# Group normalisation over 128 images: scaling shares put back on VectorE, and one load split over unequal DMA engines

## The chip, the core and the metric

The kernel runs on one core of one Trainium2 chip. The metric is the device time of one execution in microseconds (us). The core has TensorE (PE), VectorE (DVE), ScalarE (ACT), GpSimd (POOL) and SyncE (SP), and 16 DMA engines that move data between the device memory and the on-chip memory. In the profile a line number such as L368 is a line of the kernel.

## The reference

`x` has the shape (128, 1024, 32, 16) in bf16: 134 MB in, and as much out. Each image's 1024 channels form 32 groups of 32 channels. Each group of an image is normalised by its own mean and variance, and each channel is then scaled and shifted:

```
xr = x.reshape(B, G, C // G, H, W)                   # B=128, G=32
mu = xr.mean(axis=(2, 3, 4), keepdims=True)
var = ((xr - mu) ** 2).mean(axis=(2, 3, 4), keepdims=True)
xn = ((xr - mu) / sqrt(var + 1e-5)).reshape(B, C, H, W)
return xn * g[None, :, None, None] + b[None, :, None, None]
```

## The kernel before

The work is cut into 32 tiles (`NT`). A tile is four images: its 128 partitions are 4 images x 32 groups, and a partition holds one whole group, 32 channels of 512 values, which is a row of 16,384 bf16 values or 32 KB. A tile is thus 4 MB, loaded whole, changed in place and stored whole. Six buffers (`XBUFS`) rotate in `xpool`.

Loads and stores are all issued by SyncE. `L(i)` loads tile i. Six tiles are loaded up front; after that tile i+5 (`AHEAD`) is loaded after the store of tile i. Since its buffer is that of tile i-1, SyncE waits, before it issues the load, for the store of tile i-1 to have landed, and everything after it in SyncE's order waits too. The first and the last tile are loaded in four column quarters; the last two tiles are stored in quarters.

Order on every engine is fixed by `chain`, which ties each instruction to the one before it under the same key ("sp", "act", "dve", "pool", "pe"). The program writes that order out: for each tile i come `Q(i)`, `M(i+1)`, `R0(i+1)`, `V(i)`, `A(i)`.

- `M` sums the row on TensorE: 32 matmuls with an identity matrix (`eye`) add up the 32 blocks of 512 columns in PSUM (`pa`). Only the first and last tile (`shifted`) use two sums, `pa` of 8 matmuls and `pb` of 24.
- `R0` reduces that sum on VectorE to the negative mean (`negmean`, L189). For the two shifted tiles it is a quarter's estimate `q`, and `R1` adds the rest and forms a correction (`off`, `seed`) on GpSimd.
- `Q` squares the row on ScalarE with a running sum, in two halves of 8192 values whose unused outputs are FP8 (`ja`, L244). Between the halves stands `finish(i-1)`: ScalarE scales the last two channels of the tile before (`LAST_SHARE`, L363), the tile is stored and the next load issued. GpSimd then forms part of the variance (`v0`, L273).
- `V` takes the root on ScalarE and the reciprocal on VectorE (`rstd`, L312), and GpSimd forms the 32 factors and offsets of the channels (`scl` L337, `shift` L343, `bia` L353).
- `A` scales and shifts the channels in place (L368): channels 0 to 21 on VectorE, and 22 to 29 on GpSimd (`POOL_SHARE` = 8). The tile before the last is scaled wholly on VectorE, the last one on VectorE and ScalarE.

Of the kernel before, what the change touches and what calls it, by code (L numbers as in the profile page):

```python
# [8 lines left out]
ACT = mybir.ActivationFunctionType  # L9
# [3 lines left out]
FP8 = mybir.dt.float8e5  # L13
# [11 lines left out]
LAST_SHARE = 2  # L25
POOL_SHARE = 8
# [3 lines left out]
def kernel(  # L30
# [62 lines left out]

    def L(i):
        xt = xpool.tile([P, F], BF16, name="xt")
        parts = NQ if i == 0 or i >= NT - 1 else 1
        w = F // parts
        for c in range(parts):
            chain(
                "sp",  # L100
                nc.sync.dma_start(  # L101
                    out=xt[:, c * w : (c + 1) * w], in_=x_v[i][:, c * w : (c + 1) * w]
                ),
            )
        state[i] = {"xt": xt}

    for i in range(min(UPFRONT, NT)):
        L(i)

# [48 lines left out]
    def shifted(i):  # L158
        return i == 0 or i == NT - 1

    def matmuls(st, name, lo, hi):
        ps = pspool.tile([P, MMN], F32, name=name)
        for k in range(lo, hi):
            chain(
                "pe",
                nc.tensor.matmul(  # L166
                    out=ps[:],
                    lhsT=eye[:],
                    rhs=st["xt"][:, k * MMN : (k + 1) * MMN],
                    start=(k == lo),  # L170
                    stop=(k == hi - 1),
                ),
            )
        st[name] = ps

    def M(i):
        st = state[i]
        if shifted(i):
            matmuls(st, "pa", 0, MQ)
            matmuls(st, "pb", MQ, NMM)  # L180
        else:
            matmuls(st, "pa", 0, NMM)
# [18 lines left out]
    def R0(i):  # L201
        st = state[i]
        if shifted(i):
            st["q"] = sum_of(st["pa"], None, "q")
        else:
            st["negmean"] = sum_of(st["pa"], None, "negmean")

    def R1(i):
        st = state[i]
        if not shifted(i):  # L210
            return
# [3 lines left out]
            "pool",  # L215
            nc.gpsimd.tensor_scalar(  # L216
# [10 lines left out]
            "pool",  # L227
            nc.gpsimd.tensor_scalar(
                out=seed[:],
                in0=off[:],  # L230
                scalar1=-1.0,
                scalar2=off[:],
# [6 lines left out]
    def squares(st, w, k, bias, scale, sq):  # L239

        ja = jpool.tile([P, F // 2], FP8, name="ja")
        chain(
            "act",
            nc.scalar.activation(  # L244
                out=ja[:, 0:w],
                in_=st["xt"][:, k * w : (k + 1) * w],
                func=ACT.Square,
                bias=bias,
                scale=scale,
                accum_out=sq,  # L250
                saturate=False,
            ),
        )

    def Q(i):

        st = state[i]
        if shifted(i):
            sq = spool.tile([P, NQ], F32, name="sq")
            for k in range(NQ):  # L260
                squares(st, QF, k, st["q"][:], 1.0 / NQ, sq[:, k : k + 1])
                if k == 0:
                    finish(i - 1)
            st["sq"] = sq
            return
        s0 = spool.tile([P, 1], F32, name="s0")
        s1 = spool.tile([P, 1], F32, name="s1")
        squares(st, F // 2, 0, st["negmean"][:], 1.0, s0[:])
        v0 = spool.tile([P, 1], F32, name="v0")
        finish(i - 1)  # L270
        chain(
            "pool",
            nc.gpsimd.tensor_scalar(  # L273
                out=v0[:],
                in0=s0[:],
                scalar1=inv_n,
                scalar2=EPS,
                op0=ALU.mult,
                op1=ALU.add,
            ),  # L280
        )
        squares(st, F // 2, 1, st["negmean"][:], 1.0, s1[:])
        st["v0"], st["s1"] = v0, s1

    def V(i):
        st = state[i]
        if shifted(i):
            var = spool.tile([P, 1], F32, name="var")
            jv = spool.tile([P, NQ], F32, name="jv")
            chain(  # L290
                "dve",
                nc.vector.tensor_scalar(  # L292
                    out=jv[:],
                    in0=st["sq"][:],
                    scalar1=inv_n,
                    scalar2=st["seed"][:],
                    op0=ALU.mult,
                    op1=ALU.add,
                    accum_out=var[:],
                ),  # L300
            )
            last_sum, scale, bias = var, float(NQ * NQ), eps_t
        else:
            last_sum, scale, bias = st["s1"], inv_n, st["v0"]
        rstd = spool.tile([P, 1], F32, name="rstd")
        chain(
            "act",
            nc.scalar.activation(  # L308
                out=rstd[:], in_=last_sum[:], func=ACT.Sqrt, bias=bias[:], scale=scale
            ),  # L310
        )
        chain("dve", nc.vector.reciprocal(out=rstd[:], in_=rstd[:]))  # L312
        scl = spool.tile([P, KC], F32, name="scl")
        bia = spool.tile([P, KC], F32, name="bia")
        if i == NT - 1:
            chain(
                "dve",
                nc.vector.tensor_scalar(
                    out=scl[:], in0=gam, scalar1=rstd[:], scalar2=None, op0=ALU.mult
                ),  # L320
            )
            chain(
                "dve",
                nc.vector.scalar_tensor_tensor(  # L324
                    out=bia[:],
                    in0=scl[:],
                    scalar=st["negmean"][:],
                    in1=bet,
                    op0=ALU.mult,
                    op1=ALU.add,  # L330
                ),
            )
        else:
            shift = spool.tile([P, KC], F32, name="shift")
            chain(
                "pool",
                nc.gpsimd.tensor_scalar(  # L337
                    out=scl[:], in0=gam, scalar1=rstd[:], scalar2=None, op0=ALU.mult
                ),
            )  # L340
            chain(
                "pool",
                nc.gpsimd.tensor_scalar(  # L343
                    out=shift[:],
                    in0=scl[:],
                    scalar1=st["negmean"][:],
                    scalar2=None,
                    op0=ALU.mult,
                ),
            )  # L350
            chain(
                "pool",
                nc.gpsimd.tensor_tensor(out=bia[:], in0=shift[:], in1=bet, op=ALU.add),  # L353
            )
        st["scl"], st["bia"] = scl, bia

    def scale_on(key, i, k):
        st = state[i]
        span = st["xt"][:, k * HW : (k + 1) * HW]
        scl = st["scl"][:, k : k + 1]  # L360
        bia = st["bia"][:, k : k + 1]
        if key == "act":
            inst = nc.scalar.activation(  # L363
                out=span, in_=span, func=ACT.Identity, bias=bia, scale=scl
            )
        else:
            eng = nc.vector if key == "dve" else nc.gpsimd
            inst = eng.tensor_scalar(  # L368
                out=span,
                in0=span,  # L370
                scalar1=scl,
                scalar2=bia,
                op0=ALU.mult,
                op1=ALU.add,
            )
        chain(key, inst)
# [9 lines left out]

    def in_parts(i):
        return i >= NT - STORE_IN_PARTS

    def A(i):  # L390

        if not in_parts(i):
            for n in range(POOL_SHARE):
                scale_on("pool", i, KC - LAST_SHARE - POOL_SHARE + n)
            for k in range(KC - LAST_SHARE - POOL_SHARE):
                scale_on("dve", i, k)
            if i + 1 < NT:
                R1(i + 1)
            return
        for c in range(NQ):  # L400
            for k in range(c * KQ, (c + 1) * KQ):
                on_act = i == NT - 1 and k >= (c + 1) * KQ - ACT_SHARE
                scale_on("act" if on_act else "dve", i, k)
            S(i, c, c + 1)
            if c == NQ // 2 - 1 and i + 1 < NT:
                R1(i + 1)

    def finish(i):
        if i < 0 or in_parts(i):
            return  # L410
        for k in range(KC - LAST_SHARE, KC):
            scale_on("act", i, k)
        S(i, 0, NQ)
        state.pop(i)
        j = i + AHEAD
        if UPFRONT <= j < NT:
            L(j)
# [5 lines left out]
    for i in range(NT):  # L423
# [5 lines left out]
        A(i)  # L429
# [30 lines left out]
```

## Time and profile before

| What | Value |
|---|---|
| Time, median of 3 runs | 635.33 us (635.27 to 635.8) |
| The profiled execution's own time | 635.33 us |
| Its span, first to last instruction | 633.4 us |
| Bytes over the span | 268.69 MB at 424 GB/s |
| Busy: ScalarE | 518.1 us (82%) |
| Busy: VectorE | 368.9 us (58%) |
| Busy: TensorE | 289.4 us (46%) |
| Busy: GpSimd | 228.4 us (36%) |
| A load of 4 MB, issue to landing (median) | 29.2 us |
| A store of 4 MB, issue to landing (median) | 38.3 us |

Busy time is an average over the run: an engine may be the limit in one stretch and idle in the next. The queues of the DMA engines are listed by number in the page: q1 is SyncE's, q10 is the one that carried the two small loads of `g` and `b`, and q8 and q14 carry the engines' own instructions. Every row of a tile is one DMA packet. A transfer has landed when each of the DMA engines that worked on it has reported its share done.

### The profile page before, as it was taken

To read this page: it belongs to the slowest core of one execution; us is meant where nothing else is said; L and a number is where in the kernel's file an instruction comes from. 1 tells how busy PE (TensorE), PEld (TensorE's weight loads), DVE (VectorE), ACT (ScalarE), POOL (GpSimd) and SP (SyncE) were. 2 spreads that over 40 slices of the span, in tenths; PEclk is the share of its full clock that TensorE was granted. 3 is DMA by queue.
4 is the path that set the end of the run, shared out by engine and by line. 5 is a ranking of instruction groups with operands and counts; after the bars stand their busy time and mean duration, and the time that the engine had idled before them with its cause. 6 is when DMAs were issued, how large, how long until landed. Compare 5 with 4: busy or idle time off the path is not lost.

```text
span 633.4 us, 3906 instructions
## 1 busy us (share of the span) xinstructions
PE 289.4 (46%) x1025; PEld 113.3 (18%) x1025; DVE 368.9 (58%) x825; ACT 518.1 (82%) x238; POOL 228.4 (36%) x373
## 2 busy tenths in 40 slices
PE   5577604663345633456423655235553355547000
PEld 2223201221112211122101222012221122212000
DVE  0077777767744577545675455754557645567760
ACT  4599999999977798777987788977879778797960
POOL 0044444444442244422444333443324433244100
PEclk9789758766787667876668776687866678668655
DMA  9999999999999999999999999999999999999995
GB/s 367 433 431 419 430 431 430 430 433 430 430 434 433 435 431 429 431 430 428 431 435 426 433 439 439 431 426 433 430 435 430 430 435 430 433 423 439 431 418 228
DMA packets 11062, 268.69 MB, mean 424 GB/s; under 512 B 1312, under 2 KB 1312, under 8 KB 1312
## 3 DMA queue, kind: packets, MB, share of 16 engines
q1 hardware_dynamic: 10944, 268.44, 98.8%
q8 instruction: 8, 0.13, 0.1%
q14 instruction: 14, 0.11, 0.0%
q10 hardware_dynamic: 96, 0.00, 0.0%
HBM read 134.22 MB, written 134.22 MB: 424 GB/s over the span
## 4 chain that ended last, share of the span: by engine, by line
DMA 71%; ACT 10%; PE 9%; DVE 3%; issue 3%; POOL 1%; SPq 0%; DVEq 0%; ACTq 0%; POOLq 0%
DMA out_dram<-xt 41%; DMA xt<-in_x_dram 30%; PE pa L166 9%; ACT ja L244 9%; DVE xt L368 3%; ACT xt L363 1%; SPq L101 0%; POOL scl L337 0%; PE pb L166 0%; POOL shift L343 0%; ACT rstd L308 0%; DVE jd L189 0%; DVE rstd L312 0%; POOL bia L353 0%; DVE jv L292 0%
## 5 line engine op out<-in xcount | busy, mean ns | idle before, releaser
L244 ACT ACTIVATE ja<-xt,negmean 128x8192 fp8e5<-128x8192 bf16 x60 | 426.7, 7112 | 74.7 <-DVE jd L189 74.7
L166 PE MATMUL pa<-xt,eye 128*128 128x512 bf16 x976 | 278.6, 456 | 294.6 <-DMA xt<-in_x_dram 294.6
L368 DVE TENSOR_SCALAR xt<-xt,scl,bia 128x512 bf16<-128x512 bf16 x716 | 341.3, 552 | 39.8 <-POOL bia L353 39.8
L166 PEld LDWEIGHTS <-eye 128*128 128x128 bf16 x1024 | 113.2, 113 | 470.8 <-DMA xt<-in_x_dram 295.9
L368 POOL TENSOR_SCALAR xt<-xt,scl,bia 128x512 bf16<-128x512 bf16 x240 | 190.5, 805 | 3.3
L337 POOL TENSOR_SCALAR scl<-gb,rstd 128x32 f32<-128x32 f32 x31 | 11.1, 358 | 337.0 <-DVE rstd L312 337.0
L189 DVE TENSOR_SCALAR_CACHE_REDUCE jd<-pa 128x512 bf16<-128x512 f32 x32 | 22.0, 688 | 172.3 <-PE pa L166 172.3
L363 ACT ACTIVATE xt<-xt,bia,scl 128x512 bf16<-128x512 bf16 x68 | 50.8, 798 | 0.8 <-DVE bia L324 0.8
L244 ACT ACTIVATE ja<-xt,q 128x4096 fp8e5<-128x4096 bf16 x8 | 29.7, 3708 | 7.0 <-DVE jd L189 6.8
L312 DVE RECIPROCAL rstd<-rstd 128x1 f32<-128x1 f32 x32 | 5.1, 160 | 24.6 <-ACT rstd L308 24.6
L343 POOL TENSOR_SCALAR shift<-scl,negmean 128x32 f32<-128x32 f32 x31 | 11.1, 358 | 3.1
L166 PE MATMUL pb<-xt,eye 128*128 128x512 bf16 x48 | 11.0, 379 | 1.0 <-DMA xt<-in_x_dram 1.0
L244 ACT ACTIVATION_READ_ACCUMULATOR ja<-xt,negmean 128x1 f32 x60 | 11.2, 186 | 0.0
L308 ACT ACTIVATE rstd<-s,v 128x1 f32<-128x1 f32 x30 | 8.8, 295 | 2.8
L353 POOL TENSOR_TENSOR bia<-shift,gb 128x32 f32<-128x32 f32 x31 | 7.8, 251 | 2.6
L216 POOL TENSOR_SCALAR off<-negmean,q 128x1 f32<-128x1 f32 x2 | 0.9, 430 | 20.6 <-DVE jd L189 20.6
L308 ACT ACTIVATE rstd<-var,eps_t 128x1 f32<-128x1 f32 x2 | 0.6, 294 | 7.5 <-DVE jv L292 7.5
L273 POOL TENSOR_SCALAR v<-s 128x1 f32<-128x1 f32 x30 | 5.7, 191 | 2.5
L156 DVE COPY gb<-gb_p 128x64 f32<-128x64 f32 x1 | 0.2, 225 | 5.3 <-PE gb_p L148 5.3
L116 ACT ACT_TABLE_LOAD x1 | 1.3, 1283 | 1.7 <-PEq L444 1.7
L189 DVE DVE_READ_ACCUMULATOR jd<-pa 128x1 f32 x32 | 2.6, 81 | 0.0
L292 DVE TENSOR_SCALAR_CACHE_REDUCE jv<-sq,seed 128x4 f32<-128x4 f32 x2 | 0.4, 216 | 2.9 <-ACT ja L244 2.9
(18 smaller groups left out, 6.1 us busy)
## 6 DMA issues: line engine op xcount, KB each, us to landing
xt<-in_x_dram SPq DMA_DIRECT2D x30, 4096.0 KB, 29.2
out_dram<-xt SPq DMA_DIRECT2D x30, 4096.0 KB, 38.3
xt<-in_x_dram SPq DMA_DIRECT2D x8, 1024.0 KB, 16.4
out_dram<-xt SPq DMA_DIRECT2D x8, 1024.0 KB, 18.8
gb_b<-in_g_dram ACTq DMA_DIRECT2D x1, 2.0 KB, 3.4
gb_b<-in_b_dram ACTq DMA_DIRECT2D x1, 2.0 KB, 5.4
```

Source lines behind the costliest of these rows:

```text
L116: chain("act", nc.scalar.activation(out=warm[:], in_=eps_t[:], func=ACT.Sqrt))
L166: nc.tensor.matmul(out=ps[:], lhsT=eye[:], rhs=st["xt"][:, k * MMN : (k + 1) * MMN], start=(k == lo), stop=(k == hi - 1),),
L189: nc.vector.tensor_scalar(out=jd[:], in0=ps[:], scalar1=-inv_n, scalar2=seed, op0=ALU.mult, op1=ALU.add, accum_out=total[:],),
L244: nc.scalar.activation(out=ja[:, 0:w], in_=st["xt"][:, k * w : (k + 1) * w], func=ACT.Square, bias=bias, scale=scale, accum_out=sq, satura ...
L273: nc.gpsimd.tensor_scalar(out=v0[:], in0=s0[:], scalar1=inv_n, scalar2=EPS, op0=ALU.mult, op1=ALU.add,),
L308: nc.scalar.activation(out=rstd[:], in_=last_sum[:], func=ACT.Sqrt, bias=bias[:], scale=scale),
L312: chain("dve", nc.vector.reciprocal(out=rstd[:], in_=rstd[:]))
L337: nc.gpsimd.tensor_scalar(out=scl[:], in0=gam, scalar1=rstd[:], scalar2=None, op0=ALU.mult),
L343: nc.gpsimd.tensor_scalar(out=shift[:], in0=scl[:], scalar1=st["negmean"][:], scalar2=None, op0=ALU.mult,),
L353: nc.gpsimd.tensor_tensor(out=bia[:], in0=shift[:], in1=bet, op=ALU.add),
L363: inst = nc.scalar.activation(out=span, in_=span, func=ACT.Identity, bias=bia, scale=scl)
L368: inst = eng.tensor_scalar(out=span, in0=span, scalar1=scl, scalar2=bia, op0=ALU.mult, op1=ALU.add,)
```

## The change

The scaling, the small arithmetic and the squares change place, and the load of one tile is issued differently.

- `A` scales all 32 channels of a tile on VectorE (in the last tile ScalarE keeps two of every eight). `POOL_SHARE`, `LAST_SHARE` and `finish` are gone, so the store and the next load are issued after `A(i)`.
- `V` and `R1` do their small arithmetic on VectorE: `scl`, `bia`, `off`, `seed`.
- Every tile is summed and squared the way the first and the last were: `pa` of 8 matmuls gives `q`, ScalarE squares four quarters of 4096 values around `q` with bf16 outputs, and `R1(i+1)`, which needs `pb`, stands in the middle of `A(i)`.
- The load of tile 16 is issued in four parts: rows 0 to 59 by GpSimd, and rows 60 to 123, 124 to 126 and 127 by SyncE. In the change's own words the 60 rows go over 15 DMA engines, sparing engine 3, and the others over 16, 3 and 1 engines.
- `turn(n)` is a small GpSimd load of n x 4 pieces of 4 bytes from `g`, whose data nothing uses. `turn(4)` is issued after the loads up front, `turn(13)` after the split load.

```diff
-FP8 = mybir.dt.float8e5
-LAST_SHARE = 2
-POOL_SHARE = 8
+SPLIT_TILE = 16
+WIDE = 60
+SPARED = 3
...
+    def turn(n):
+        t = consts.tile([n, 4, 4], BF16, name=f"turn{n}")
+        chain("pool", nc.gpsimd.dma_start(
+                out=t[:, :, 0:2],
+                in_=g[0 : n * 8].rearrange("(p a c) -> p a c", a=4, c=2)))
...
     def L(i):
         xt = xpool.tile([P, F], BF16, name="xt")
+        if i == SPLIT_TILE:
+            chain("pool", nc.gpsimd.dma_start(
+                    out=xt[0:WIDE, :], in_=x_v[i][0:WIDE, :], max_dma_last_dim=2 * F))
+            for lo, hi in ((WIDE, P - 4), (P - 4, P - 1), (P - 1, P)):
+                chain("sp", nc.sync.dma_start(out=xt[lo:hi, :], in_=x_v[i][lo:hi, :]))
+            turn(16 - SPARED)
+            state[i] = {"xt": xt}
+            return
...
     for i in range(min(UPFRONT, NT)):
         L(i)
+
+    turn(SPARED + 1)
...
     def M(i):
         st = state[i]
-        if shifted(i):
-            matmuls(st, "pa", 0, MQ)
-            matmuls(st, "pb", MQ, NMM)
-        else:
-            matmuls(st, "pa", 0, NMM)
+        for name, lo, hi in (("pa", 0, MQ), ("pb", MQ, NMM)):
...
     def Q(i):
+        sq = spool.tile([P, NQ], F32, name="sq")
+        for k in range(NQ):
+            ja = jpool.tile([P, QF], BF16, name="ja")
+            chain("act", nc.scalar.activation(out=ja[:],
+                    in_=st["xt"][:, k * QF : (k + 1) * QF], func=ACT.Square,
+                    bias=st["q"][:], scale=1.0 / NQ, accum_out=sq[:, k : k + 1]))
-        squares(st, F // 2, 0, st["negmean"][:], 1.0, s0[:])
-        finish(i - 1)
-        chain("pool", nc.gpsimd.tensor_scalar(out=v0[:], in0=s0[:], ...))
-        squares(st, F // 2, 1, st["negmean"][:], 1.0, s1[:])
...
     def V(i):
-        chain("pool", ...)      # scl, shift, bia
+        chain("dve", ...)       # scl, bia
...
+    def A(i, c):
+        for k in range(c * KQ, (c + 1) * KQ):
+            if i == NT - 1 and k >= (c + 1) * KQ - ACT_SHARE:
+                chain("act", nc.scalar.activation(...))
+            else:
+                chain("dve", nc.vector.tensor_scalar(...))
...
         V(i)
-        A(i)
+        in_parts = i >= NT - STORE_IN_PARTS
+        for c in range(NQ):
+            A(i, c)
+            if in_parts:
+                S(i, c, c + 1)
+            if c == NQ // 2 - 1 and i + 1 < NT:
+                R1(i + 1)
+        if not in_parts:
+            S(i, 0, NQ)
+        state.pop(i)
+        j = i + AHEAD
+        if UPFRONT <= j < NT:
+            L(j)
```

More of the change, by code (lines that the diff above doesn't have):

```diff
@@ L92 @@
     state = {}
+    def turn(n):
+        t = consts.tile([n, 4, 4], BF16, name=f"turn{n}")
+        chain(
+            "pool",
+            nc.gpsimd.dma_start(
+                out=t[:, :, 0:2],
+                in_=g[0 : n * 8].rearrange("(p a c) -> p a c", a=4, c=2),
+            ),
+        )
     def L(i):
         xt = xpool.tile([P, F], BF16, name="xt")
+        if i == SPLIT_TILE:
+            chain(
+                "pool",
+                nc.gpsimd.dma_start(
+                    out=xt[0:WIDE, :], in_=x_v[i][0:WIDE, :], max_dma_last_dim=2 * F
+                ),
+            )
+            for lo, hi in ((WIDE, P - 4), (P - 4, P - 1), (P - 1, P)):
+                chain(
+                    "sp", nc.sync.dma_start(out=xt[lo:hi, :], in_=x_v[i][lo:hi, :])
+                )
+            turn(16 - SPARED)
+            state[i] = {"xt": xt}
+            return
         parts = NQ if i == 0 or i >= NT - 1 else 1
@@ L156, in GB @@
         chain("dve", nc.vector.tensor_copy(out=gb[:], in_=gb_p[:]))
[L158 to L174, printed above, removed]
     def M(i):
         st = state[i]
-        if shifted(i):
-            matmuls(st, "pa", 0, MQ)
-            matmuls(st, "pb", MQ, NMM)
-        else:
-            matmuls(st, "pa", 0, NMM)
+        for name, lo, hi in (("pa", 0, MQ), ("pb", MQ, NMM)):
+            ps = pspool.tile([P, MMN], F32, name=name)
+            for k in range(lo, hi):
+                chain(
+                    "pe",
+                    nc.tensor.matmul(
+                        out=ps[:],
+                        lhsT=eye[:],
+                        rhs=st["xt"][:, k * MMN : (k + 1) * MMN],
+                        start=(k == lo),
+                        stop=(k == hi - 1),
+                    ),
+                )
+            st[name] = ps
     def sum_of(ps, seed, name):
@@ L201, in R0 @@
     def R0(i):
[L202 to L206, printed above, removed]
+        state[i]["q"] = sum_of(state[i]["pa"], None, "q")
     def R1(i):
         st = state[i]
-        if not shifted(i):
-            return
         st["negmean"] = sum_of(st["pb"], st["q"][:], "negmean")
@@ L214, in R1 @@
         chain(
-            "pool",
-            nc.gpsimd.tensor_scalar(
+            "dve",
+            nc.vector.tensor_scalar(
                 out=off[:],
@@ L226, in R1 @@
         chain(
-            "pool",
-            nc.gpsimd.tensor_scalar(
+            "dve",
+            nc.vector.scalar_tensor_tensor(
                 out=seed[:],
                 in0=off[:],
-                scalar1=-1.0,
-                scalar2=off[:],
+                scalar=-1.0,
+                in1=off[:],
                 op0=ALU.mult,
@@ L237, in R1 @@
         st["seed"] = seed
-    def squares(st, w, k, bias, scale, sq):
-        ja = jpool.tile([P, F // 2], FP8, name="ja")
-        chain(
[L243 to L251, printed above, removed]
-            ),
-        )
[L255 to L262, printed above, removed]
-                    finish(i - 1)
[L264 to L267, printed above, removed]
-        squares(st, F // 2, 0, st["negmean"][:], 1.0, s0[:])
[L269 to L281, printed above, removed]
-        squares(st, F // 2, 1, st["negmean"][:], 1.0, s1[:])
-        st["v0"], st["s1"] = v0, s1
@@ L285, in V, with Q @@
[L285 to L304, printed above, removed]
+    def Q(i):
+        st = state[i]
+        sq = spool.tile([P, NQ], F32, name="sq")
+        for k in range(NQ):
+            ja = jpool.tile([P, QF], BF16, name="ja")
+            chain(
+                "act",
+                nc.scalar.activation(
+                    out=ja[:],
+                    in_=st["xt"][:, k * QF : (k + 1) * QF],
+                    func=ACT.Square,
+                    bias=st["q"][:],
+                    scale=1.0 / NQ,
+                    accum_out=sq[:, k : k + 1],
+                ),
+            )
+        st["sq"] = sq
@@ L305, in V @@
+    def V(i):
+        st = state[i]
+        var = spool.tile([P, 1], F32, name="var")
+        jv = spool.tile([P, NQ], F32, name="jv")
+        chain(
+            "dve",
+            nc.vector.tensor_scalar(
+                out=jv[:],
+                in0=st["sq"][:],
+                scalar1=inv_n,
+                scalar2=st["seed"][:],
+                op0=ALU.mult,
+                op1=ALU.add,
+                accum_out=var[:],
+            ),
+        )
         rstd = spool.tile([P, 1], F32, name="rstd")
@@ L308, in V @@
             nc.scalar.activation(
-                out=rstd[:], in_=last_sum[:], func=ACT.Sqrt, bias=bias[:], scale=scale
+                out=rstd[:],
+                in_=var[:],
+                func=ACT.Sqrt,
+                bias=eps_t[:],
+                scale=float(NQ * NQ),
             ),
@@ L314, in V @@
         bia = spool.tile([P, KC], F32, name="bia")
[L315 to L372, printed above, removed]
+        chain(
+            "dve",
+            nc.vector.tensor_scalar(
+                out=scl[:], in0=gam, scalar1=rstd[:], scalar2=None, op0=ALU.mult
+            ),
+        )
@@ L373, in scale_on @@
+        chain(
+            "dve",
+            nc.vector.scalar_tensor_tensor(
+                out=bia[:],
+                in0=scl[:],
+                scalar=st["negmean"][:],
+                in1=bet,
                 op0=ALU.mult,
                 op1=ALU.add,
-            )
-        chain(key, inst)
+            ),
+        )
+        st["scl"], st["bia"] = scl, bia
+    def A(i, c):
+        st = state[i]
+        xt = st["xt"]
+        for k in range(c * KQ, (c + 1) * KQ):
+            span = xt[:, k * HW : (k + 1) * HW]
+            scl = st["scl"][:, k : k + 1]
+            bia = st["bia"][:, k : k + 1]
+            if i == NT - 1 and k >= (c + 1) * KQ - ACT_SHARE:
+                chain(
+                    "act",
+                    nc.scalar.activation(
+                        out=span, in_=span, func=ACT.Identity, bias=bia, scale=scl
+                    ),
+                )
+            else:
+                chain(
+                    "dve",
+                    nc.vector.tensor_scalar(
+                        out=span,
+                        in0=span,
+                        scalar1=scl,
+                        scalar2=bia,
+                        op0=ALU.mult,
+                        op1=ALU.add,
+                    ),
+                )
@@ L385, in S @@
         )
[L387 to L417, printed above, removed]
     M(0)
```

## The prediction

> **What bounds the kernel now.** I read the page's DMA parts first, then the chain of waits, SyncE's own waits, the tail of the run in stretches, and last the trace's completion records.
>
> ```profile
> span 633.4 us, 3906 instructions
> ...
> DMA  9999999999999999999999999999999999999995
> ...
> q1 hardware_dynamic: 10944, 268.44, 98.8%
> q8 instruction: 8, 0.13, 0.1%
> q14 instruction: 14, 0.11, 0.0%
> ```
>
> The DMA engines are full in 39 of 40 slices, and nearly all they carry is x in and out. No computing engine is as full (ACT 82%, DVE 58%). SyncE's own waits say the same: it waits for earlier stores to land and free a buffer, hardly for results.
>
> ```profile
> SPq L101 <- DMA out_dram<-xt: 451.3, 26, 19.5
> SPq L381 <- DVE xt L368: 125.7, 16, 36.8
> ```
>
> So time can only come from how many rows each DMA engine moves and what else it does. The last stretches (columns: length, five engines, clock, DMA share, GB/s) show how unevenly they finish:
>
> ```profile
> 620.00:622.00 2.00, 0.00 (x0) 0.00 (x0) 0.00 (x0) 0.00 (x0) 0.00 (x0) 0.50 1.01 426
> 622.00:624.00 2.00, 0.00 (x0) 0.00 (x0) 0.00 (x0) 0.00 (x0) 0.00 (x0) 0.50 0.96 406
> 624.00:626.00 2.00, 0.00 (x0) 0.00 (x0) 0.00 (x0) 0.00 (x0) 0.00 (x0) 0.50 0.62 262
> 626.00:628.00 2.00, 0.00 (x0) 0.00 (x0) 0.00 (x0) 0.00 (x0) 0.00 (x0) 0.50 0.26 111
> 628.00:630.00 2.00, 0.00 (x0) 0.00 (x0) 0.00 (x0) 0.00 (x0) 0.00 (x0) 0.50 0.13 53
> 630.00:632.00 2.00, 0.00 (x0) 0.00 (x0) 0.00 (x0) 0.00 (x0) 0.00 (x0) 0.50 0.06 25
> ```
>
> A share of 0.06 is one engine of 16: for the last 2 us a single engine works, at 25 GB/s. The trace also keeps, for each transfer, sixteen completion times, one per engine. For the transfers below, first completion (us) and how far behind it the six latest engines came:
>
> ```
>  22.27   0.38 0.39 0.40 0.42 0.43 0.59
>  71.45   0.41 0.42 0.44 0.50 2.03 2.70
> 216.73   1.55 1.60 2.64 3.58 4.16 4.34
> 313.55   2.51 2.56 3.41 4.45 5.08 5.95
> 400.71   2.74 3.36 3.97 4.37 5.01 6.90
> 623.75   2.34 3.28 3.39 4.41 5.04 6.27 8.65   (last transfer, seven latest)
> ```
>
> One engine loses 8.65 us on the fastest over the run, the next 6.27. It steps down where an 8 KB instruction packet lies. Packets of that size on q14 at 225.4, 313.5, 402.6, 499.1 and 593.2 us are each followed by a step of 0.78 to 0.97 us of the same last engine. They are about 90 us apart, 128 VectorE instructions; the other groups on q14 (three 160 to 180 us apart, three about 250 us) fit GpSimd and ScalarE. The packet takes 0.31 us, and the row after it is 0.38 to 0.66 us longer than the usual 1.213 us. From 4.34 behind at 217 us to 8.65 at the end, five packets: **0.86 us each**. The kernel ends when VectorE's instruction-fetching DMA engine ends.
>
> **Part by part.** *Scaling back on VectorE.* GpSimd's 240 scalings and 127 small operations, ScalarE's 60 scalings and both FP8 half-tile squares go; VectorE scales 32 channels a tile instead of 22 and does the small arithmetic.
>
> ```profile
> 575.27 10.77 DVE L368 TENSOR_SCALAR xt<-xt,scl,bia 128x512 bf16<-128x512 bf16 x22 [1.28 <-POOL bia L353]
> 575.34 6.35 POOL L368 TENSOR_SCALAR xt<-xt,scl,bia 128x512 bf16<-128x512 bf16 x8
> ...
> 591.54 5.25 DVE L368 TENSOR_SCALAR xt<-xt,scl,bia 128x512 bf16<-128x512 bf16 x16 [1.28 <-POOL bia L353]
> ```
>
> With GpSimd scaling beside it a VectorE scaling averages 0.49 us here (0.55 over the run); alone it takes 5.25/16 = 0.328. VectorE per tile: 32 x 0.328 = 10.5, two sums 0.69 + 0.74 with their read-outs 0.16, `jv` 0.30, `rstd` 0.16, `scl` 0.24, `bia` 0.25, `off` and `seed` at most the 0.43 and 0.29 that GpSimd took: 13.8 us. ScalarE: four squares of 3.71 + 0.19 and a root of 0.29: 15.9 us. A tile has two transfers of 9.71 us (first completions 22.27 and 31.98), 19.4 us. Both fit, so I cost the computing at nothing. Its cover is the DMA queue: the store issued at 280.41 had its last scaling at 272.7, 7.7 us of slack. The changed order needs only 8 of 32 matmuls (3.5 us instead of 9) before VectorE may go on, so stores become ready some 4 us earlier than now. If that cover were gone, every microsecond over 19.4 would count 31 times.
>
> *More VectorE instructions.* Section 1's 825 and 72 waits, branches and drains make 897 now; the built program has 1443. At one packet per 128, first at the 64th, that is 7 packets now and 11 after. Four more at 0.86: **+3.44 us** on the engine that is already last (bounds 4 x 0.78 = 3.1 and 4 x 0.97 = 3.9). GpSimd's packets vanish, but from engines that are not last: nothing for the end.
>
> [...]
>
> *The split load.* A row is 32 KB and costs its engine 9.71/8 = 1.214 us. A plain load gives each engine 8 rows. Now, by the change's words, 60 rows go as 4 rows on 15 engines, 64 as 4 on 16, and the last four as one each on three engines and one more on one. Engine 3 has 4 rows and saves 4 x 1.214 = **-4.86 us**; if the single row falls on one of the three, they have 10, 9 and 9, and pay 2.43, 1.21 and 1.21. Engine numbers are not in the trace; I take 3 to be the last engine, and the three to be none of the late ones, and weigh the contrary below.
>
> [...]
>
> *The second queue's own cost.* No data row goes from GpSimd now, so I bound it. Low: the 64-byte packets of `gb_b` on q10 between rows cost 0.01 us, and most 8 KB rows after them took 0.309, as elsewhere. High: each of the four rows lengthens the next one as an instruction packet does at its worst, 4 x 0.66 = 2.6 us on the fifteen engines. A gain is excluded: the bytes stay. I take 0.5, one lengthening, since the four follow one another. The next engine then stands at 6.27 + 0.5 = 6.8.
>
> *Waits and issues.* GpSimd's load waits for tile 10's store, as SyncE's did; only the small `turn(13)` queues behind it. Two more SyncE issues at about 0.35 us precede tile 12's store, which has the slack above. The first `turn` precedes `eye` on GpSimd and may hold up the first matmuls; tile 0's store, issued at 45.15 us, has loads ahead of it until 64 us.
>
> *Sum.* Last engine: 8.65 + 3.44 - 4.86 = 7.23 us behind, above 6.8, so it still ends last, 1.42 us sooner. Span 633.4 - 1.4 = 632.0; the profiled execution took 635.33, 1.93 more than its span, and equals the median of three: **633.9 us**.
>
> **Rivals.** *The second queue is dear.* If the fifteen pay 2.6, the second engine comes to 8.9 (+0.2); if the one at 6.27 is also loaded with 1.21 to 2.43 more, to 10.1 or 11.3: 635.6 to 638.0 us. For: the long rows after instruction packets. Against: q10's cheap packets.
>
> *The wrong engine is spared.* This ends slower. Then VectorE's fetches go unpaid: +3.44, 638.8 us (638.4 to 639.2). It decides if the engine without rows is any but the last one. For: no number in the trace ties it to 3. [...]
>
> *VectorE becomes the bound.* If scalings stayed at 0.552 us without GpSimd beside them, 32 of them and 3.3 us make 21 us a tile against 19.4: about 50 us more. The 0.328 rows speak against it.
>
> **Numbers.** Forecast 0.62, its own range 632.9 (the last engine is passed by the one at 6.27) to 635.4 (that engine is the one with two rows more, at 8.7); dear queue 0.18; wrong engine 0.17; VectorE 0.03. Low 632.9; high 638.8, since without half of the third case too much is left out. 0.2% is 1.27 us, about what can be told from no change. Of the forecast 0.38 lies below 634.06, 0.22 within and 0.02 above the bound; the dear queue gives 0.06 same and 0.12 slower; the others are slower.
>
> **What would show it.** Right: about fifteen q14 instruction packets; a GpSimd queue with 60 rows; VectorE scalings near 0.33 us; a last transfer whose engines spread over about 7.2 us, with the one-engine stretch shorter; tile 16's load short on one engine only. Wrong: the last engine steps down 11 times and never recovers (wrong engine); a common step of all but one engine near tile 16's load (dear queue); idle DMA slices mid-run (computing).

## The result, and the profile after

The changed kernel takes 646.3 us (median of 4 runs, 644.04 to 647.31) against 635.49 us for the kernel before on the same chip: 1.0165 times as long, 95% interval 1.0138 to 1.0192. The forecast was 633.9 us, with a range from 632.9 to 638.8. The profiled execution took 647.31 us with a span of 645.6 us, so the span grew by 12.2 us.

The page of the changed kernel, whose GB/s row has the moved bytes in 40 equal slices of 16.1 us:

```profile
span 645.6 us, 4013 instructions
...
GB/s 378 435 420 418 424 440 427 427 441 428 426 434 435 424 439 427 382 329 349 435 432 430 433 435 432 431 430 439 429 432 435 431 429 439 428 418 439 432 413 143
...
q1 hardware_dynamic: 10888, 266.47, 97.2%
q0 software_dynamic: 144, 1.97, 1.1%
q8 instruction: 8, 0.13, 0.1%
q14 instruction: 15, 0.12, 0.0%
```

Fifteen instruction packets on q14 and 1.97 MB (60 rows) on a new queue are as foreseen. Not foreseen are the slices 17 to 19, at 382, 329 and 349 GB/s where all others in the middle are near 431. Against 431 that is (49 + 102 + 82)/431 x 16.1 = 8.7 us of lost transfer. Tile 16's load is issued at 262 us, and the bytes fall from 268 us on. In stretches of 4 us (last two columns: DMA share, GB/s):

```profile
260.00:264.00 4.00, 0.95 (x5) 0.22 (x3) 3.93 (x14) 3.97 (x3) 1.17 (x2) 1.00 1.04 451
264.00:268.00 4.00, 0.00 (x0) 0.00 (x0) 4.00 (x14) 3.97 (x4) 0.00 (x0) 0.76 1.13 418
268.00:272.00 4.00, 0.00 (x0) 0.00 (x0) 1.21 (x4) 3.97 (x4) 0.00 (x0) 0.50 0.87 270
272.00:276.00 4.00, 0.00 (x0) 0.00 (x0) 0.00 (x0) 0.00 (x1) 0.00 (x0) 0.50 1.01 319
...
284.00:288.00 4.00, 4.00 (x14) 1.58 (x13) 1.89 (x9) 1.49 (x2) 0.00 (x0) 0.68 1.07 279
288.00:292.00 4.00, 3.31 (x16) 1.28 (x14) 4.00 (x14) 3.97 (x3) 0.00 (x0) 1.00 1.10 229
292.00:296.00 4.00, 0.00 (x0) 0.00 (x0) 3.93 (x14) 3.97 (x3) 0.00 (x0) 0.67 0.75 213
...
304.00:308.00 4.00, 4.00 (x20) 1.85 (x19) 3.53 (x14) 3.33 (x2) 0.00 (x0) 1.00 1.01 434
```

The DMA share stays near 1 (0.75 to 1.13 in these stretches) while the bytes fall to half: the engines are not short of work, each row takes longer. The packet records say the same. GpSimd's 60 rows, with rows of a store between them, took 1.9 us each in the median. Near 286 us, when they have all gone, most rows of SyncE's 64-row part take 2.48 to 2.50 us, and a few later ones up to 4.5, where a row elsewhere takes 1.213. Two dips of unlike make, one with GpSimd's queue and one without, are a first hint that the queue is not the cause.

At the end one engine works alone for longer than before, at 25 to 29 GB/s from 638 us on:

```profile
634.00:636.00 2.00, 0.00 (x0) 0.00 (x0) 0.00 (x0) 0.00 (x0) 0.00 (x0) 0.50 0.46 193
636.00:638.00 2.00, 0.00 (x0) 0.00 (x0) 0.00 (x0) 0.00 (x0) 0.00 (x0) 0.50 0.21 90
638.00:640.00 2.00, 0.00 (x0) 0.00 (x0) 0.00 (x0) 0.00 (x0) 0.00 (x0) 0.50 0.06 25
640.00:642.00 2.00, 0.00 (x0) 0.00 (x0) 0.00 (x0) 0.00 (x0) 0.00 (x0) 0.50 0.07 29
642.00:644.00 2.00, 0.00 (x0) 0.00 (x0) 0.00 (x0) 0.00 (x0) 0.00 (x0) 0.50 0.07 29
```

The sixteen completions of the last transfer now spread over 15.6 us instead of 8.65, and the last engine still steps back by about a microsecond after VectorE's instruction packets (from 5.24 to 6.24 us behind after the one at 242.1 us, from 16.30 to 17.26 after the one at 527.0).

### The profile page after: what moved, and what is told of

Same layout as the page of the kernel before. It is cut to its first block, busy times and chain, and to the rows that moved or that the text cites. A ratio compares the mean times of both kernels' runs of the same rounds, so it can differ in the third digit from the quotient of the medians.

```text
span 645.6 us, 4013 instructions
## 1 busy us (share of the span) xinstructions
PE 291.2 (45%) x1025; PEld 113.6 (18%) x1025; DVE 412.8 (64%) x1371; ACT 500.0 (77%) x298; POOL 2.7 (0%) x9
## 3 DMA queue, kind: packets, MB, share of 16 engines
q0 software_dynamic: 144, 1.97, 1.1%
## 4 chain that ended last, share of the span: by engine, by line
DMA 76%; ACT 11%; DVE 4%; PE 2%; issue 2%; SPq 1%; DVEq 0%; ACTq 0%
DMA out_dram<-xt 59%; DMA xt<-in_x_dram 17%; ACT ja L258 11%; DVE xt L335 3%; PE pa L192 2%; SPq L126 1%; DVE jv L275 0%; ACT rstd L288 0%; DVE bia L307 0%; DVE jd L207 0%; DVE scl L301 0%; DVE rstd L296 0%; DVEq L402 0%; ACTq L258 0%; SPq L348 0%
## 5 line engine op out<-in xcount | busy, mean ns | idle before, releaser
L258 ACT ACTIVATE ja<-xt,q 128x4096 bf16<-128x4096 bf16 x128 | 474.2, 3705 | 10.0 <-DVE jd L207 6.8
L335 DVE TENSOR_SCALAR xt<-xt,scl,bia 128x512 bf16<-128x512 bf16 x1016 | 333.7, 407 | 1.2
L192 PE MATMUL pa<-xt,eye 128*128 128x512 bf16 x256 | 110.0, 608 | 307.1 <-DMA xt<-in_x_dram 307.1
L192 PE MATMUL pb<-xt,eye 128*128 128x512 bf16 x768 | 187.4, 404 | 0.0
L288 ACT ACTIVATE rstd<-var,eps_t 128x1 f32<-128x1 f32 x32 | 9.4, 294 | 106.1 <-DVE jv L275 106.1
L258 ACT ACTIVATION_READ_ACCUMULATOR ja<-xt,q 128x1 f32 x128 | 23.8, 186 | 0.0
L207 DVE TENSOR_SCALAR_CACHE_REDUCE jd<-pb,q 128x512 bf16<-128x512 f32 x32 | 23.8, 744 | 0.0
L307 DVE SCALAR_TENSOR_TENSOR bia<-scl,negmean,gb 128x32 f32<-128x32 f32 x32 | 8.1, 252 | 1.1
L301 DVE TENSOR_SCALAR scl<-gb,rstd 128x32 f32<-128x32 f32 x32 | 7.7, 242 | 1.1
L328 ACT ACTIVATE xt<-xt,bia,scl 128x512 bf16<-128x512 bf16 x8 | 5.8, 800 | 0.8 <-DVE bia L307 0.8
```

Source lines behind the costliest of these rows:

```text
L192: nc.tensor.matmul(out=ps[:], lhsT=eye[:], rhs=st["xt"][:, k * MMN : (k + 1) * MMN], start=(k == lo), stop=(k == hi - 1),),
L207: nc.vector.tensor_scalar(out=jd[:], in0=ps[:], scalar1=-inv_n, scalar2=seed, op0=ALU.mult, op1=ALU.add, accum_out=total[:],),
L258: nc.scalar.activation(out=ja[:], in_=st["xt"][:, k * QF : (k + 1) * QF], func=ACT.Square, bias=st["q"][:], scale=1.0 / NQ, accum_out=sq[: ...
L288: nc.scalar.activation(out=rstd[:], in_=var[:], func=ACT.Sqrt, bias=eps_t[:], scale=float(NQ * NQ),),
L301: nc.vector.tensor_scalar(out=scl[:], in0=gam, scalar1=rstd[:], scalar2=None, op0=ALU.mult),
L307: nc.vector.scalar_tensor_tensor(out=bia[:], in0=scl[:], scalar=st["negmean"][:], in1=bet, op0=ALU.mult, op1=ALU.add,),
```

## The experiments

Three theories. **P**: a load cut by rows is slow in itself, because of which partitions are written together. **Q**: rows on GpSimd's queue beside SyncE's are slow. **C**: the all-VectorE arrangement costs the time. Besides, the spared engine may not be the late one. Every kernel but the last is built on the changed one; the kernel before ran beside all of them.

**Without the split.** Tile 16 is loaded like any other.

```diff
-        if i == SPLIT_TILE:
-            ...
-    turn(SPARED + 1)
```

> The changed kernel with tile 16 loaded whole by SyncE again and without the two small GpSimd loads. Theory P (a load cut by rows is slow in itself: in the changed kernel's trace rows of the 64-row part take 2.48 us instead of 1.21) and theory Q (rows on GpSimd's queue beside SyncE's are slow) both expect the mid-run dip to go and 638 to 640 us: the four more instruction packets of VectorE at 0.86 us, +3.4. Theory C (the all-VectorE arrangement itself costs the time) expects 645 or more.

Measured: 638.59 us against 635.05, ratio 1.0056 (1.0041 to 1.0071). C falls. The dip is gone, as the GB/s row shows. The arrangement costs 3.5 us, close to the forecast's 3.44 for four more instruction packets, and nearly all of it at the end, on one engine:

```profile
GB/s 367 447 432 397 440 433 431 432 429 428 428 430 434 434 434 431 427 430 433 440 434 430 427 434 432 438 432 435 427 430 434 423 437 432 436 415 443 428 417 135
...
626.00:628.00 2.00, 0.00 (x0) 0.00 (x0) 0.00 (x0) 0.00 (x0) 0.00 (x0) 0.50 0.19 82
628.00:630.00 2.00, 0.00 (x0) 0.00 (x0) 0.00 (x0) 0.00 (x0) 0.00 (x0) 0.50 0.06 25
...
634.00:636.00 2.00, 0.00 (x0) 0.00 (x0) 0.00 (x0) 0.00 (x0) 0.00 (x0) 0.50 0.05 20
```

The last transfer's last completion comes 11.82 us after its first (8.65 before, 12.09 foreseen). From 217 us on the last engine steps back seven times, where it did five times before, each time at a packet on q14 that fits VectorE's count of instructions (242.4, 300.2, 359.3, 417.2, 460.3, 518.2 and 575.4 us). The split itself therefore costs 646.3 - 638.6 = 7.7 us, or 10.8 - 3.5 = 7.3 when each kernel is set against the kernel before on its own chip.

**Halves by rows, halves by columns, and a whole load by GpSimd.** These three change only tile 16's load of the kernel without the split; the new lines of each:

```diff
+        if i == SPLIT_TILE:    # row halves
+            for lo, hi in ((0, 64), (64, P)):
+                chain("sp", nc.sync.dma_start(out=xt[lo:hi, :], in_=x_v[i][lo:hi, :]))
+        if i == SPLIT_TILE:    # column halves
+            for lo, hi in ((0, F // 2), (F // 2, F)):
+                chain("sp", nc.sync.dma_start(out=xt[:, lo:hi], in_=x_v[i][:, lo:hi]))
+        if i == SPLIT_TILE:    # whole, by GpSimd
+            chain("pool", nc.gpsimd.dma_start(out=xt[:], in_=x_v[i], max_dma_last_dim=2 * F))
```

> The kernel without the split, but tile 16 loaded by two SyncE loads of rows 0 to 63 and 64 to 127. P: each of an engine's 8 rows takes 2.48 instead of 1.21 us, +10 us on the kernel without the split, rows at 2.4 to 2.5 us. Q: no difference from it, within 1 us. [...]

> As before, but tile 16 loaded by two SyncE loads of all 128 rows and half of the columns each. [...] If cutting a load costs by itself, +1 us or more.

> The kernel without the split, with tile 16 loaded whole by GpSimd. P: all 128 rows on their usual engines, so no difference from the kernel without the split, within 1.5 us, though single rows may take up to 2.4 us while two queues take turns on an engine. Q: +5 to +10 us and a dip of the throughput near 265 us.

Measured on the same chip: row halves 645.85 us (ratio to before 1.017, 1.0155 to 1.0186), column halves 638.21 (1.0049, 1.0034 to 1.0064), whole by GpSimd 638.43 (1.0053, 1.0036 to 1.007). Row halves, all on SyncE, cost 7.3 us over the kernel without the split; the other two cost nothing. Q falls, and of P it stands that the cut by rows is slow; why it is slow comes below. The stretches of row halves:

```profile
272.00:276.00 4.00, 4.00 (x10) 1.36 (x10) 0.49 (x1) 0.50 (x2) 0.00 (x0) 0.50 1.08 410
276.00:280.00 4.00, 3.95 (x15) 1.60 (x15) 3.53 (x15) 3.62 (x2) 0.00 (x0) 0.77 1.16 287
280.00:284.00 4.00, 1.89 (x9) 0.68 (x7) 3.93 (x14) 3.97 (x3) 0.00 (x0) 1.00 0.85 180
284.00:288.00 4.00, 0.00 (x0) 0.00 (x0) 4.00 (x14) 3.97 (x4) 0.00 (x0) 0.58 0.99 213
```

of column halves:

```profile
280.00:284.00 4.00, 0.64 (x3) 0.10 (x1) 3.93 (x14) 3.97 (x3) 0.00 (x0) 0.85 0.98 418
284.00:288.00 4.00, 2.19 (x6) 0.82 (x7) 4.00 (x14) 3.97 (x3) 0.00 (x0) 0.50 1.07 459
```

and of the whole load by GpSimd, issued at about 262 us:

```profile
264.00:268.00 4.00, 0.00 (x0) 0.00 (x0) 4.00 (x14) 3.97 (x3) 0.00 (x0) 0.50 0.99 426
268.00:272.00 4.00, 0.00 (x0) 0.00 (x0) 0.57 (x2) 3.43 (x2) 0.00 (x0) 0.50 1.05 451
272.00:276.00 4.00, 0.34 (x1) 0.13 (x2) 0.00 (x0) 0.00 (x0) 0.00 (x0) 0.50 0.99 426
```

**The four parts on SyncE, and eighths by rows.**

```diff
+            for lo, hi in ((0, WIDE), (WIDE, P - 4), (P - 4, P - 1), (P - 1, P)):   # parts
+            for lo, hi in [(16 * n, 16 * n + 16) for n in range(8)]:                # eighths
+                chain("sp", nc.sync.dma_start(out=xt[lo:hi, :], in_=x_v[i][lo:hi, :]))
```

> The changed kernel's four parts of tile 16 (60, 64, 3 and 1 rows), all issued by SyncE, without the small GpSimd loads. P: like the changed kernel, 644 to 648 us, since the same partitions are written together. Q: like the kernel without the split, 638 to 640 us, apart from the unequal row counts. Which engine is left out of the 60 rows may differ.

> The kernel without the split, with tile 16 loaded by eight SyncE loads of 16 rows each, one row per engine and load. [...] Q: no difference, +2 us at most for the issues. If only the cut in two matters, about +10 us.

The four parts on SyncE take 647.55 us (1.0185, 1.0168 to 1.0202), like the change itself: the loss does not need GpSimd's queue. Eighths take 654.59 us (two runs; 1.0302, 1.0276 to 1.0327), 16 us over the kernel without the split. That is twice the cost of halves, in P's direction: rows took 3.1 to 4.0 us, at 131 to 172 GB/s:

```profile
280.00:284.00 4.00, 0.32 (x2) 0.00 (x0) 3.93 (x14) 3.94 (x4) 0.00 (x0) 1.00 1.24 172
284.00:288.00 4.00, 0.00 (x0) 0.00 (x0) 4.00 (x14) 3.97 (x3) 0.00 (x0) 0.66 0.98 139
...
296.00:300.00 4.00, 0.00 (x0) 0.00 (x0) 0.00 (x0) 0.00 (x0) 0.00 (x0) 0.50 0.97 131
```

**On chip or in the device memory?** Row halves differ from column halves on both sides: fewer partitions on chip, and half the address range in the device memory. This kernel reads as row halves do and writes as column halves do.

```diff
+            for h in range(2):
+                chain("sp", nc.sync.dma_start(
+                    out=xt[:, h * F // 2 : (h + 1) * F // 2],
+                    in_=x_v[i][h * 64 : h * 64 + 64, :].rearrange("r (u c) -> (r u) c", u=2)))
```

> The kernel without the split, tile 16 loaded by two SyncE loads, each from 64 rows of the input (as the load in row halves) but into all 128 partitions and half the columns (as the load in column halves). Tile 16's values thus stand in other rows, so its part of the output is not the reference's. If the cost of row halves lies on chip, where few partitions are written together: no cost, 638 to 639 us, rows of 16 KB at 0.61 us. If it lies in the device memory, where only half of a tile's range is read at a time: 645 to 646 us as with row halves.

Measured: 637.85 us (1.004, 1.0025 to 1.0056), no cost, and no dip:

```profile
276.00:280.00 4.00, 4.00 (x18) 1.72 (x17) 3.54 (x12) 3.97 (x3) 0.00 (x0) 0.93 0.97 418
280.00:284.00 4.00, 1.06 (x5) 0.29 (x3) 3.93 (x14) 3.94 (x4) 0.00 (x0) 0.92 1.01 434
284.00:288.00 4.00, 1.92 (x5) 0.74 (x6) 4.00 (x14) 3.97 (x3) 0.00 (x0) 0.50 1.03 438
```

So the cost lies on the side of the partitions. One difference remains untested: this load moves packets of 16 KB and row halves packets of 32 KB. Column halves show only that packets of 16 KB cost nothing of themselves. With row halves the rate fell to 180 to 213 GB/s (280 to 288 us), half of the usual 431 or a little less; with parts of 16 partitions it was 131 to 172 (280 to 300 us), far above an eighth of 431 (54). What on the chip makes parts with fewer partitions slower, no run shows.

**Which engine is late, and which was spared?** Extra copies of n half rows are put into SyncE's queue behind one tile's store each. Each of those listed below ended with n completions, read as one per engine, so an engine shows itself at the step where it joins. The traces hold no engine numbers: a number here is the place, counted from 0, in the order in which longer copies take engines.

```diff
+            n = i - LADDER
+            if 1 <= n <= 15:
+                at = n * (n - 1) // 2
+                chain("sp", nc.sync.dma_start(out=o_v[NT - 1][at : at + n, 0 : F // 2],
+                                              in_=x_v[NT - 1][at : at + n, 0 : F // 2]))
```

> The kernel without the split, with an extra copy of n half rows (16 KB each) from the input to rows of the output that the last tile's store overwrites later, after the store of tile 10 + n, for n = 1 to 15. If a transfer of n rows runs on the n lowest engines, one row each, the engine numbered f gains about 0.6 us or more of delay in each step with n over f. The number of steps in which the last engine (the one with VectorE's instruction packets) is delayed tells its number: 12 steps for engine 3. If it is engine 3, the changed kernel's load did not spare the engine that it names; if it is another, the change spared an engine that was not last.

Completions of the copies in the trace, first one's time and the distances from it, in us. One that each copy reports about 1 us after its issue, long before the rest, is left out:

```
n = 3   314.48   0  0.46  0.98
n = 4   334.45   0  0.46  0.98  6.61
n = 5   354.43   0  0.47  1.67  1.70  7.40
n = 6   373.93   0  0.48  0.94  2.15  2.86  7.88
```

The late engine is absent at n = 3 and there from n = 4 on: it is the fourth in that order, engine 3. If the change counts the engines in the same order, it names the right one. (The run, with its extra copies, took 645.87 us.)

> The changed kernel with the extra copies of n half rows, n = 1 to 12, after the store of tile 17 + n. [...] VectorE's instruction-fetching engine must join at n = 4 again. If GpSimd's 60 rows spared engine 3, that same engine would also be the one that came out of tile 16's load ahead of the rest; if they spared another, the engine that is ahead joins at another step, or at none up to 12 if its number is 12 or more.

> The changed kernel with extra copies of n half rows after tiles 18 to 22, n = 11 to 15. The engine that came out of tile 16's load ahead joined in none of the steps 1 to 11, so it has a number of 11 or more; the step at which a completion some 4 us ahead of the others appears tells it. If none up to 15 has one, it is engine 15: GpSimd's 60 rows then went over the fifteen lowest engines, not over fifteen from engine 4 on.

> The same without the two small GpSimd loads (turn). If they move the place at which GpSimd's 60 rows begin, another engine is now ahead after tile 16's load, and it joins at another step. If they do nothing, the same engine is ahead and the time is within 1% of the run with them.

On the changed kernel engine 3 joins at n = 4 again, 9.36 us behind the first. The engine that left tile 16's load ahead, 3 to 4 us before all others, joins in none of the steps up to 11 (652.5 us), nor in 12 to 15 (651.24 us). At n = 15 the numbers are these: the store just before is completed first at 491.97 us by the engine ahead and 3.59 us later by the next; the copy is completed first at 496.17, 4.20 us after that store's first, which is the next engine's 3.59 and 0.61 for its half row. The engine ahead does not run the 15-row copy. It is the sixteenth in the same order, engine 15. Without the small GpSimd loads the time is 652.26 us, and again the engine ahead is missing at n = 15 (3.76 = 3.16 + 0.60). So the 60 rows went over engines 0 to 14, with the small loads and without them, and engine 3 had its full share. The small loads were meant to set the engine at which the 60 rows begin. With them and without them the sixteenth engine was left out; why, the runs do not show.

**A version with fewer VectorE instructions.** Since packets on engine 3 set the end, the kernel before is given more GpSimd work.

```diff
-POOL_SHARE = 8
+POOL_SHARE = 15
```

> The kernel before with POOL_SHARE 15 in place of 8: seven more channels of a tile move from VectorE to GpSimd. VectorE then has 688 instructions of all kinds in place of 897, 5 instruction packets in place of 7. If the last engine is set by them: 2 x 0.86 = 1.7 us less, the engine at 6.27 just behind it, 633.4 to 634.2 us. If the scalings of both engines become too slow together (15 of GpSimd at 0.8 us are 12 us a tile, against 19.4): 636 us or more, with idle DMA slices.

Measured: 634.01 us against 635.18, ratio 0.9982 (0.9973 to 0.9991): 1.2 us less than the kernel before, and within the 633.4 to 634.2 us expected. GpSimd is busy 394.1 us instead of 228.4, and no DMA slice in the middle falls. The last completion comes 7.11 us after the first, with the next engine at 7.01, and the one-engine stretch is gone. The engine at 7.01 is the one that still steps back (near 420 and 541 us); the one at 7.11 slips little by little, so still fewer packets would gain little here:

```profile
626.00:628.00 2.00, 0.00 (x0) 0.00 (x0) 0.00 (x0) 0.00 (x0) 0.00 (x0) 0.50 0.37 156
628.00:630.00 2.00, 0.00 (x0) 0.00 (x0) 0.00 (x0) 0.00 (x0) 0.00 (x0) 0.50 0.16 66
630.00:632.00 2.00, 0.00 (x0) 0.00 (x0) 0.00 (x0) 0.00 (x0) 0.00 (x0) 0.50 0.02 8
```

## Why the prediction was wrong

- **What bounds the kernel: right.** The end is that of the DMA engine on which VectorE's instruction packets fall: with more of them it came later, with fewer sooner. The copies of n rows place it fourth, as engine 3. One reading was loose: the line with 125.7 us of waits for L368 is not "hardly for results". All but 2.0 us of them lie before 120 us and after 560; between, SyncE waits 422.5 us for stores, so what was concluded holds.
- **More VectorE instructions: right.** +3.44 us foreseen, 3.5 measured alone: 11.82 - 8.65 = 3.2 on the last engine, and 0.4 on all (the last transfer's first completion, 624.13 against 623.75).
- **Scaling on VectorE at no cost: right.** Sixteen scalings without GpSimd beside them took 5.26 us, 0.329 each, and without the split no DMA slice in the middle emptied.

```profile
305.76 5.26 DVE L335 TENSOR_SCALAR xt<-xt,scl,bia 128x512 bf16<-128x512 bf16 x16
```

- **The second queue's own cost: near enough and beside the point.** It was put at 0.5 us; a whole load by GpSimd cost nothing (638.43 us against 638.59). The sign named for a dear queue did appear, all engines but one falling back near tile 16's load; but the four parts on SyncE lost as much, so the sign does not tell the two causes apart.
- **The split load: wrong, and this is the step that failed, twice.** It priced a row at 1.214 us whatever else is in flight. A part of 60 or 64 rows lies all or nearly all in one half of the partitions, and its rows took 1.9 to 2.5 us: 7.3 to 7.7 us for the one tile. The same bytes cut by columns cost nothing. No case of the forecast held this, so the range ended below the result. And it took the 4.86 us of engine 3 as saved, which were not; engine 15 was spared. The rival of the wrong engine was thus true of the engine. Its 638.8 us, which also puts the split's rows at nothing, is what the kernel without the split takes (638.59); the loss that decided was another.
- **Why the halves cost 7.3 us.** Rows at 2.48 us, eight per engine, would cost 8 x 1.27 = 10 us. With row halves the last transfer's first completion does come 9.1 us later than without the split (633.20 against 624.13), but its last only 7.3 (643.20 against 635.95). The last engine is 7.32 us behind the first when the first half lands and 4.90 when the second does, at 298.95 us, and rows that begin after 295 us take 1.2 us again, all but a few. So the last engine passed its last rows of the split load at the usual price, when the other engines were through.
- **Left open.** No run tried a split that really spares engine 3, so what that would gain is not known.

## What to carry to other kernels

When the DMA engines are full, price a transfer by the partitions that it touches together, not only by bytes per engine: here a load cut into row halves moved at half rate (180 to 213 GB/s) where the same bytes cut by columns moved at full rate (418 and 459). Check which engine a transfer really leaves out before paying for it; copies of n rows, put one after the other into a queue, show in the completion times at which n an engine joins. And count instructions per engine: where they are fetched through one of the busy DMA engines, moving work to another computing engine can shorten the end, here by 1.2 us.

## What the runs showed of the hardware

An 8 KB instruction packet of VectorE cost its DMA engine about 0.9 us (before, from 4.34 to 8.65 us behind in five packets), nearly three times its 0.31 us of transfer. These packets fell on one engine in 16: the same last engine stepped back after each of the five from 217 us on before, and after each of the seven without the split. The 16 KB packets on q8, 246 to 260 TensorE instructions apart, fell on changing engines: before, after those at 256.7, 414.0, 491.4 and 568.8 us, an engine that had been among the foremost fell back by 1.3 to 1.6 us, each time another one. A small load meant to move GpSimd's place among the engines moved nothing: with 60 rows the same engine, the sixteenth to join, was left out both with it and without it. While parts of 64 partitions of a load were in flight, the core's rate fell to 180 to 213 GB/s, with parts of 16 partitions to 131 to 172; with the load cut by columns it stayed at the usual 430 or so.
